# Where the spread of w_out's greatest row scale is written in an attention and feed-forward kernel

## The chip, the cores and the metric

One Trainium2 chip; the program runs on one of its cores. The metric is the device time of an execution in microseconds, and what stands for a kernel is the median of its runs. The kernel before was run three times: 697.34, 698.10 and 700.95 us.

## The reference, cut to what matters

```python
# B, H, S, D = 4, 8, 576, 64; d_model 512, d_ff 2048
x = (log1p(abs(i - j)) / log1p(max(i, 1)))[..., None]
bias = maximum(x @ w1 + b1, 0.0) @ w2              # one table for each head
scores = q @ k.T / 8 + bias
attn = exp(scores - scores.max(-1)); attn = attn / (attn.sum(-1) + 1e-9)
x = (attn @ v).transpose(0, 2, 1, 3).reshape(B * S, H * D)
h = x @ w_in                                       # w_in, w_out are float64
return ((h * clip(h + 3.0, 0.0, 6.0) / 6.0) @ w_out).astype(float32)
```

## The kernel before, in words

**Tiles and steps.** The attention is cut into 144 tiles of 128 query rows of one head, in pairs of heads: first the query columns 0 to 255 of all four batches (`u` = 0, four tiles for a pair), then the columns 256 to 575 (`u` = 1, five tiles). A loop at the end of the kernel function counts `n` from -1 to 150 (L1146). In turn n, `front(n)` writes the scores of tile n + 1, the row maximum of tile n, and what the tiles n - 1 to n - 6 still need; then come steps of the preparation of the weights, of the bias table and of the feed-forward part, and last `back(n)` with the exponential. The tiles of the batches 0 and 1 with u = 0 are computed in float32 and turned by TensorE (L614, L656); the others are split into high and low float16 parts and turned by DMA transposes on SP (L631).

**The feed-forward part.** `ffn(b, u)` is a generator (L728). It has 16 steps that each write 12 matmuls of `x @ w_in` into a PSUM tile `h_ps` (L773), with `post` (L745) turning an older `h_ps` into `t` (ScalarE L763, VectorE L756) and `g` (ScalarE L750, GpSimd L752). Then come 16 steps of 12 matmuls of `g @ w_out` into `o_ps` (L796), four for each of the four groups of output rows. The first one, `ffn(0, 0)`, stops between its halves with `yield "w2"` (L785): its second half needs the prepared `w_out`, and before the first `o_ps` it multiplies the sixteen `g` by the row ratios of `w_out` (L787, by turns on ScalarE L123 and VectorE L121).

**The preparation of w_out.** `w_out_prep` (L328) is a generator too. Its stages, for eight blocks k of two times 128 rows, are: load, sign (L256, L257), pack, split. `pack` (L354) shifts the float64 words together, takes the greatest value of each row (L264) and makes a power of two and its inverse of it (`row_scale`, L208, L163, L213). `split` (L359) writes the high and the low float16 parts into `wo`, the low ones on VectorE (L140). In the twelfth step only the split of block 7 is left. Behind the stages comes `row_ratio(pw, "w2")` (L215) with the chain of `spread_max` (L144) and a `yield` after each hop: a maximum over the eight scales of each partition on VectorE (`m_w`, L146); a transpose to one row on TensorE (L152); a maximum over that row on VectorE (`g_w`, L154); a product with a row of ones, which lays the value on all partitions, on TensorE (L156); a copy out of PSUM on VectorE (`p_w`, L159). Then VectorE takes the inverse (L218) and the ratios `r_w2c` (L220), and the tables of L371. The transpose and the product write the tile `m_ps`, which comes from the pool `w` like `h_ps`, `o_ps` and `pv_ps`; that pool has two PSUM banks at this stage.

**What sets the order.** A planner orders the instructions of each engine by their place in the text and by times that it reckons itself; it may let a later one pass where an earlier one isn't ready. From n = 45 on (`SWITCH`, the entry `sw`), `open_steady` (L1111) closes the PSUM pools, opens others with two and four tiles, and TensorE goes in the order of the text; SP too, from n = 45. An engine runs its own list in order in any case. How many steps a turn writes is kept in counters:

```python
ao[0] += cfg["ro"] if out_steps[0] < cfg["os"] else cfg["ro2"]     # 0.85, then 2.0 from 11 steps on
while ao[0] >= 1.0:
    ao[0] -= 1.0
    out_ready = not out_step()                                     # the generator is at its end
...
if phase == 1.5 and not out_ready:
    credit = cfg["gap"]                                            # 0.0
else:                            # rf0 1.3; rfo 2.3; rf 2.0, and rf1 1.55 from unit 16 on (u = 1)
    credit += cfg["rf0"] if phase == 1 else cfg["rfo"] if phase < 2 else ...
while credit >= 1.0 and queue and (phase < 2 or steady[0]):        # one feed-forward step for each
```

Phase is 1 from n = 21 (`START`), 1.5 while `ffn(0, 0)` stands at its `yield "w2"` and in its second half, and 2 when it is done; until n = 45 no other `ffn` is begun. Steps of the bias table (L855, L838, L842, L871) are written at 1.7 for a turn once `out_steps` has come to 12. What the queue of feed-forward steps holds at the end of the loop is written behind it.

Of the kernel before, what the change touches and what calls it, by code (L numbers as in the profile page):

```python
# [14 lines left out]
AF = mybir.ActivationFunctionType  # L15
# [9 lines left out]
NG = S // 16  # L25
CQ = 2.0 ** -25
VC = 5 * 128
CFG = {'z0': 'AD', 'gz': 12, 'z1': 'AD', 'gz2': 16, 'zeng': 'DDA', 'sg': 'P', 'wm1': 'A', 'wm2': 'RRAAAAAA', 'hl': 'AP', 'gl': 'PP', 'vm': 'A', 'g0': 8, 'rwi': 2.0, 'rw0': 0.3, 'rw1': 0.7, 'ro': 0.85, 'rb': 1.7, 'rf0': 1.3, 'rf': 2.0, 'rf1': 1.55, 'la': 6, 'gq': 2, 'gap': 0.0, 'wu': 8, 'act': 'o', 'g1': 2, 'w64': 5, 'rfo': 2.3, 'tv': 'A', 'pw': 0, 'po': 0, 'gr': 'AD', 'wb': 3, 'fb': 2, 'spn': 45, 'sw': 45, 'ws': 2, 'kn': 10, 'kw': 1, 'os': 11, 'ro2': 2.0, 'bo': 12, 'rb0': 1.5}
F64_BIAS = 2.0 ** -112
F64_MAX = float(np.uint32(0x0FEFFFFF).view(np.float32))  # L30

# [2 lines left out]
def attention_moe_kernel(  # L34
# [16 lines left out]
    nc = tc.nc  # L51
    cfg = CFG
# [4 lines left out]
    KF = DFF // 128  # L57
# [13 lines left out]
    stack_p = ctx.enter_context(ExitStack())  # L71

    def open_psum(stack, ns, nw):
        for tag, n in (("s", ns), ("w", nw)):
            pools["ps_" + tag] = stack.enter_context(
                tc.tile_pool(
                    name=f"ps_{tag}{n}", bufs=n, space=bass.MemoryType.PSUM, reuse_waits="tile"
                )
            )
# [4 lines left out]
    phase = 0  # L84
    out_open = [False, 0]
    steady = [False]
    queue = []

    def w_bank(name):

        if name == "o_ps":
            out_open[:] = [True, 0]
        elif out_open[0] and steady[0]:
            while out_open[0] and out_open[1] == 3:
                next(queue[0])
            out_open[1] += 1
        return pools["ps_w"].tile([128, 512], F32, tag="w", name=name)
# [109 lines left out]
    def row_scale(top, p, s):  # L207
        nc.vector.tensor_scalar(  # L208
            out=p.bitcast(U32), in0=top.bitcast(U32), scalar1=3, scalar2=0x7F800000,
            op0=ALU.logical_shift_left, op1=ALU.bitwise_and,  # L210
        )
        to_pow2(p)
        nc.vector.reciprocal(out=s, in_=p)  # L213

    def row_ratio(p, name):  # L215
        pm = yield from spread_max(p, name)
        rm = const.tile([128, 1], F32, name=f"rm_{name}")
        nc.vector.reciprocal(out=rm, in_=pm)  # L218
        r = const.tile([128, p.shape[1]], F32, name=f"r_{name}c")
        nc.vector.tensor_scalar(out=r, in0=p, scalar1=rm, scalar2=None, op0=ALU.mult)  # L220
        pscale[name] = pm
        pscale["r" + name[1]] = r
# [105 lines left out]
    def w_out_prep():  # L328
        top = const.tile([128, KF // 2], F32, name="w2top")
        pw = const.tile([128, KF // 2], F32, name="w2p")  # L330
        sw = const.tile([128, KF // 2], F32, name="w2s")

        def col(t, k):
            return t[:, k:k + 1]

        def load(k):
            src = w_out[256 * k:256 * k + 256, :].rearrange("(a p) e -> p a e", a=2)
            return f64_load(src, k)

        def load_early(k, _):  # L340
            return load(k) if k < 6 else None

        def load_late(k, t):
            return load(k) if k >= 6 else t

        def sign(k, t):
            if k % 2:
                u = const.tile([128, 2 * S], F32, tag="kb1", name="cu")
            else:
                u = pools["e"].tile([128, 2 * S], F32, tag="cu", name="cu")  # L350
            u = u[:, 0:1024]
            return (*f64_abs(t, u), u)

        def pack(k, tu):  # L354
            f64_pack(*tu[:3], col(top, k))
            row_scale(col(top, k), col(pw, k), col(sw, k))
            return tu[3].rearrange("p (k e) -> p k e", k=2)

        def split(k, u):  # L359
            ks = slice(2 * k, 2 * k + 2)  # L360
            for step in range(2):
                split_w(wo[:, 0, ks, :], wo[:, 1, ks, :], u, col(sw, k), step, pick("wm2", k))

        ws = cfg["ws"]
        yield from staged(KF // 2, [
            (0, load_early), (ws - 1, load_late), (ws, sign), (ws + 1, pack), (ws + 2, split),
        ])
        yield from row_ratio(pw, "w2")
        for name, c in (("t3", 3.0 * CQ), ("t6", 6.0 * CQ)):
            t = const.tile([128, KF // 2], F32, name=name)  # L370
            nc.vector.tensor_scalar(  # L371
                out=t, in0=pscale["r2"], scalar1=c, scalar2=None, op0=ALU.mult
            )
            pscale[name] = t
# [298 lines left out]
    def x_first(b, p):  # L673
        ps = pv_t.pop((b, p, 0))
        n = 256
        x = x_tile(b, 0)
        xr = hl_p.tile([128, 2, n], F32, tag="hl", name="xr")
        xs, rb = xr[:, 0], xr[:, 1]
        nc.scalar.activation(
            out=rb, in_=ps[:, 1, 0:n], func=AF.Copy,  # L680
            scale=pscale["x1"][:, p:p + 1] if b else pscale["v0"][1],
        )
        nc.vector.tensor_mul(out=xs, in0=ps[:, 0, 0:n], in1=rb)  # L683
        xh = x[:, 0, p]
        nc.scalar.activation(out=xh, in_=xs, func=AF.Copy)
        nc.gpsimd.tensor_sub(out=x[:, 1, p], in0=xs, in1=xh)
# [137 lines left out]
    bias_ps = {}  # L824
# [19 lines left out]
        bias_z[g] = zs  # L844

    def bias_mm(g):
        if steady[0]:
            pss = [w_bank("b_ps") for _ in range(2)]
        else:
            ps = s_bank("b_ps")  # L850
            pss = [ps[:, 0], ps[:, 1]]
        zs = bias_z.pop(g)
        for a in range(2):
            for k, z in enumerate(zs):
                nc.tensor.matmul(  # L855
                    out=pss[a][32 * k:32 * k + 32, 0:HALF], lhsT=w2_sb,
                    rhs=z[:, a * HALF:(a + 1) * HALF],
                )
        bias_ps[g] = pss if steady[0] else ps

    def bias_out(g):
        ps = bias_ps.pop(g)
# [59 lines left out]
    def front(n):  # L922
        late = at(n + 1) and not direct(*tiles[n + 1])
        if at(n + 1) and not late:
            qk_step(n + 1)
        if at(n):
            soft_max(n)
        if n == START:
            open_ffn()
        if n == SWITCH:  # L930
            open_steady()
        if late:
            qk_step(n + 1)
        if unit_at(n - 6):
            x_low(*unit_at(n - 6))
        if at(n - 1):
            soft_norm(n - 1)
        if at(n - 2):
            soft_low(n - 2)
            if tiles[n - 2][2] in (1, 3, 5, 7, 8):  # L940
                freed[0] += 1
        if at(n):
            aux(n)
        if at(n - 3):
            soft_turn(n - 3)
        if unit_at(n - 5):
            pv_step(*unit_at(n - 5))
        while len(bt_t) - freed[0] < 4 and len(bt_t) < len(keys):
            k, b, p, i = keys[len(bt_t)]
            if k - n > (cfg["la"] if n > 3 else 2):  # L950
                break
            bias_until(128 * i + 128 if i < 2 else S)
            bt_t[b, p, i] = load_bias(b, p, i)
        if unit_at(n - 6) and unit_at(n - 6)[1] == PAIRS - 1:
            return unit_at(n - 6)[::2]
        return None
# [95 lines left out]
    def drain(gen):  # L1052
        for _ in gen:
            pass
# [34 lines left out]
    def open_ffn():  # L1089
        nonlocal phase  # L1090
        drain(gen_w)
        hidden_scale(0)
        for c in range(KC):
            xv = x_t[0, 0][:, :, c]
            nc.vector.tensor_scalar(
                out=xv, in0=xv, scalar1=pscale["r1"][:, c:c + 1], scalar2=None, op0=ALU.mult
            )
        if cfg["fb"] > 1:
            x1 = const.tile([128, KC], F32, name="x1")
            nc.vector.tensor_scalar(  # L1100
                out=x1, in0=pscale["r1"], scalar1=pscale["v1"][1], scalar2=None, op0=ALU.mult
            )
            pscale["x1"] = x1
        stack_a.close()
        del pools["a"], pools["w"]
        pools["g"] = ctx.enter_context(tc.tile_pool(name="g", bufs=1, reuse_waits="tile"))
        pools["f"] = ctx.enter_context(tc.tile_pool(name="f", bufs=2, reuse_waits="tile"))
        queue.append(ffn(0, 0))
        phase = 1

    def open_steady():  # L1111
        nonlocal phase
        while phase < 2:
            ffn_step()
        stack_p.close()
        open_psum(ctx, 2, 4)
        steady[0] = True
        keep_order("PE")

# [121 lines left out]
```

## Time and profile before

| what | us |
|---|---|
| median of three runs | 698.10 |
| lowest and highest | 697.34, 700.95 |
| profiled execution | 701.47 |
| its span, first to last instruction | 699.7 |
| TensorE busy in the span | 643.5 (92%) |
| ScalarE, VectorE, GpSimd busy | 488.1, 481.9, 254.5 |

The profile is of one execution. PE stands for TensorE's matmuls, PEld for its weight loads, DVE for VectorE, ACT for ScalarE, POOL for GpSimd, SP for the queue that issues most DMAs. A releaser behind an arrow is the instruction that ended an idle time. PEclk is the granted clock as a share of the full one (1.00 is 2.4 GHz, 0.50 is 1.2 GHz). A few per cent of the matmul records can be missing.

### The profile page before, as it was taken

What the parts mean: (1) busy time and instruction counts of PE and PEld (TensorE: products, weight loads), DVE (VectorE), ACT (ScalarE), POOL (GpSimd) and SP (SyncE); (2) the same over time, 40 slices, a digit from 0 to 9 for tenths busy, and PEclk for the clock granted to TensorE, in tenths of its full rate; (3) what the DMA queues carried; (4) which work ended last, traced back from release to release, by engine and by line L of the source; (5) the groups of instructions that cost most, each with busy time, mean ns of one, the idle gap of its engine ahead of it and who ended that gap; (6) DMA issues with size and microseconds to landing.
All of it is one profiled execution on the core that took longest, in us unless ns stands there. A gap on an engine that the chain in (4) does not pass through costs nothing. (4 is left out here: it accounts for less than half of the span.)

```text
span 699.7 us, 15119 instructions
## 1 busy us (share of the span) xinstructions
PE 643.5 (92%) x5558; PEld 456.8 (65%) x5558; DVE 481.9 (69%) x1157; ACT 488.1 (70%) x963; POOL 254.5 (36%) x322
## 2 busy tenths in 40 slices
PE   7687899775999999999898899999999999999998
PEld 2233556552576667688787788767776777777775
DVE  7989868899757786667777877777678767410310
ACT  7987778886657897677668876886678856621620
POOL 1112126774202444045434552565236512410420
PEclk9999999998799999999999999999999999999999
DMA  8899679643798949999999799969796877100000
GB/s 297 298 363 344 242 277 330 217 166 77 218 256 201 246 82 299 189 237 180 244 262 250 142 229 184 219 147 200 139 243 121 161 151 128 21 10 29 1 10 28
DMA packets 175737, 130.13 MB, mean 186 GB/s; under 512 B 137520, under 2 KB 144944, under 8 KB 174640
## 3 DMA queue, kind: packets, MB, share of 16 engines
q1 hardware_dynamic: 165872, 113.84, 65.0%
q10 hardware_dynamic: 9792, 15.34, 7.2%
q8 instruction: 43, 0.70, 0.4%
q14 instruction: 30, 0.25, 0.1%
HBM read 77.24 MB, written 15.34 MB: 132 GB/s over the span
## 5 line engine op out<-in xcount | busy, mean ns | idle before, releaser
L773 PE MATMUL h_ps<-x,wi 128*128 128x256 f16 (+1 forms) x1536 | 200.7, 289 | 15.1 <-DVE xr L683 7.4
L796 PE MATMUL o_ps<-g,wo 128*128 128x256 f16 (+1 forms) x1536 | 195.5, 286 | 1.0 <-ACT g L123 1.0
L773 PEld LDWEIGHTS <-wi 128*128 128x128 f16 x1536 | 148.0, 99 | 63.4 <-issue 21.8
L796 PEld LDWEIGHTS <-wo 128*128 128x128 f16 x1536 | 147.2, 98 | 46.9 <-issue 9.9
L752 POOL TENSOR_TENSOR g<-t,g 128x256 f16<-128x256 f32 (+1 forms) x128 | 100.4, 795 | 127.9 <-ACT g L750 126.9
L566 ACT ACTIVATE bt<-bt,sm 128x576 f32<-128x576 f32 x144 | 110.5, 768 | 51.2 <-DVE sm L555 49.0
L140 DVE SCALAR_TENSOR_TENSOR hl<-bt,sm,hl 128x576 f16<-128x576 f32 x112 | 98.6, 893 | 24.9 <-ACT hl L123 14.3
L756 DVE SCALAR_TENSOR_TENSOR t<-t,t,h_ps 128x320 f32<-128x320 f32 (+1 forms) x112 | 56.3, 515 | 66.3 <-ACT t L763 65.1
L117 POOL TENSOR_SCALAR hl<-bt,sm 128x576 f16<-128x576 f32 x56 | 45.9, 821 | 105.9 <-DVE sm L578 52.6
L750 ACT ACTIVATE g<-t 128x256 f16<-128x256 f32 (+1 forms) x128 | 55.4, 440 | 35.9 <-DVE t L756 35.2
L555 DVE CUSTOM_DVE_ANT_0 bt<-s_ps,bt 128x576 f32<-128x576 f32 x88 | 64.4, 750 | 11.8 <-PE s_ps L543 6.5
L763 ACT ACTIVATE t<-h_ps,t,hr 128x320 f32<-128x320 f32 (+1 forms) x112 | 64.6, 586 | 8.2 <-PE h_ps L773 6.9
L409 POOL TENSOR_TENSOR qkl<-st,qkh 128x576 fp32r<-128x576 f32 (+2 forms) x48 | 57.2, 1214 | 32.0 <-ACT qkh L402 26.5
L855 PE MATMUL b_ps<-z_e,w_sb 128*32 128x288 f32 x448 | 47.6, 445 | 8.5 <-ACT z_e L842 3.3
L806 ACT ACTIVATE ot<-o_ps,os 128x256 f32<-128x256 f32 (+1 forms) x32 | 15.9, 496 | 56.7 <-PE o_ps L796 54.4
L123 ACT ACTIVATE hl<-bt,sm 128x576 f16<-128x576 f32 x56 | 43.0, 769 | 5.3 <-issue 1.2
L574 DVE TENSOR_SCALAR sm<-sm 128x1 f32<-128x1 f32 x112 | 16.8, 150 | 43.2 <-ACT bt L566 42.9
L838 DVE TENSOR_SCALAR z_e<-T,nbp 128x576 f32<-128x576 f32 x69 | 37.4, 586 | 5.4 <-PE b_ps L855 5.2
L543 PE MATMUL s_ps<-qkh 64*128 64x288 f32 x192 | 30.9, 353 | 8.9 <-DVE sm L555 7.3
L842 ACT ACTIVATE z_e<-T,bp 128x576 f32<-128x576 f32 x43 | 32.2, 770 | 6.6 <-PE b_ps L855 2.9
L871 ACT ACTIVATE bo<-b_ps,cv_sb,isc 128x576 f32<-128x576 f32 (+1 forms) x47 | 33.3, 711 | 3.8 <-PE b_ps L855 2.7
L257 POOL TENSOR_SCALAR w<-w 128x1024 f32<-128x1024 f32 x8 | 11.8, 1472 | 63.0 <-ACT wo L256 57.0
(132 smaller groups left out, 891.2 us busy)
## 6 DMA issues: line engine op xcount, KB each, us to landing
bt<-bias SPq DMA_DIRECT2D x36, 576.0 KB, 5.4
bias<-bo ACTq DMA_DIRECT2D x36, 288.0 KB, 5.6
w<-in_w_in_dram SPq DMA_DIRECT2D x8, 1024.0 KB, 7.0
vs<-in_vp_dram SPq DMA_DIRECT2D x24, 320.0 KB, 5.2
st<-in_qk_dram SPq DMA_DIRECT2D x16, 448.0 KB, 4.5
wo<-in_w_out_dram SPq DMA_DIRECT2D x5, 1024.0 KB, 6.6
bt<-bias SPq DMA_DIRECT2D x16, 288.0 KB, 3.5
qk<-in_qkd_dram SPq DMA_DIRECT2D x8, 544.0 KB, 8.7
```

The lines of the kernel that those rows point to most:

```text
L117: nc.gpsimd.tensor_scalar(out=out, in0=full, scalar1=scale, scalar2=1.0, op0=ALU.mult, op1=ALU.mult)
L140: nc.vector.scalar_tensor_tensor(out=out, in0=full, scalar=scale, in1=high, op0=ALU.mult, op1=ALU.subtract)
L409: nc.gpsimd.tensor_sub(out=lo[:, c:c + w], in0=t[:, c:c + w], in1=hi[:, c:c + w].bitcast(F32))
L555: nc.vector.tensor_tensor_reduce(out=halves(bt), in0=ps, in1=halves(src), op0=ALU.add, op1=ALU.min, scale=-0.125, scalar=3.0e38, accum_out ...
L566: nc.scalar.activation(out=bt, in_=bt, func=AF.Exp, scale=-1.0, bias=sm[:, 0:1], accum_out=total)
L750: nc.scalar.activation(out=g[:, 0], in_=uu, func=AF.Copy)
L752: e.tensor_sub(out=g[:, 1], in0=uu, in1=g[:, 0])
L756: nc.vector.scalar_tensor_tensor(out=t_t[f], in0=t_t[f], scalar=cols(f)[2], in1=h_t.pop(f)[:, 0:n], op0=ALU.min, op1=ALU.mult,)
L763: nc.scalar.activation(out=t_t[f], in_=h_t[f][:, 0:n], func=AF.Relu, scale=cols(f)[0], bias=cols(f)[1],)
L773: nc.tensor.matmul(out=h_t[f][:, 0:n], lhsT=wi[:, a, c, f * 128:(f + 1) * 128], rhs=x[:, e, c], start=(k == 0), stop=(k == 3 * KC - 1),)
L796: nc.tensor.matmul(out=ops[:, 0:n], lhsT=wo[:, a, f, e * 128:(e + 1) * 128], rhs=g_t[f][:, r], start=(f == 0 and a == 0 and r == 0), stop= ...
L855: nc.tensor.matmul(out=pss[a][32 * k:32 * k + 32, 0:HALF], lhsT=w2_sb, rhs=z[:, a * HALF:(a + 1) * HALF],)
```

## The change

The row-ratio chain of `w_out` is made a generator in `pack` of the last block and drained there, so it is written in the eleventh step of `w_out_prep`, before the step with the last split. At its old place the generator is at its end and gives no more `yield`. The other new names do nothing with the values given: `psw` = 99 calls `open_banks` in a turn in which it has been called, `xp` = 0 takes the old branch, and `four` is set in the same call as `steady`.

```diff
-CFG = {..., 'bo': 12, 'rb0': 1.5}
+CFG = {..., 'bo': 12, 'rb0': 1.5, 'psw': 99, 'xp': 0, 'mw': 2}
...
+        ratio = []
...
         def pack(k, tu):
             f64_pack(*tu[:3], col(top, k))
             row_scale(col(top, k), col(pw, k), col(sw, k))
+            if k == KF // 2 - 1 and cfg["mw"]:
+                ratio.append(row_ratio(pw, "w2"))
+                if cfg["mw"] > 1:
+                    drain(ratio[0])
+                else:
+                    next(ratio[0])
             return tu[3].rearrange("p (k e) -> p k e", k=2)
...
-        yield from row_ratio(pw, "w2")
+        yield from ratio[0] if ratio else row_ratio(pw, "w2")
...
-        elif out_open[0] and steady[0]:
+        elif out_open[0] and four[0]:
...
+        if n == cfg["psw"]:
+            open_banks()
         if n == SWITCH:
             open_steady()
...
+    def open_banks():
+        if not four[0]:
+            stack_p.close()
+            open_psum(ctx, 2, 4)
+            four[0] = True
...
     def open_steady():
         nonlocal phase
         while phase < 2:
             ffn_step()
-        stack_p.close()
-        open_psum(ctx, 2, 4)
+        open_banks()
         steady[0] = True
         keep_order("PE")
```

## Rows read from the trace of the kernel before

**Rows 1.** The page: busy time, share of the span and instructions of each engine.

```profile
PE 643.5 (92%) x5558; PEld 456.8 (65%) x5558; DVE 481.9 (69%) x1157; ACT 488.1 (70%) x963; POOL 254.5 (36%) x322
```

**Rows 2.** Windows, all engines; the last three columns are granted clock, DMA share, GB/s.

```profile
core 0: us, PE busy (x) PEld busy (x) DVE busy (x) ACT busy (x) POOL busy (x), PEclk, DMA share, GB/s
169.00:182.00 13.00, 12.03 (x57) 6.12 (x58) 10.33 (x23) 7.31 (x13) 5.54 (x7) 0.50 0.97 278
...
190.00:223.00 33.00, 32.78 (x315) 24.48 (x312) 23.33 (x62) 21.92 (x40) 5.83 (x7) 1.00 0.88 226
223.00:233.00 10.00, 8.36 (x93) 4.72 (x93) 7.33 (x17) 7.41 (x13) 3.20 (x4) 0.84 1.12 220
233.00:300.00 67.00, 64.00 (x678) 48.13 (x676) 46.98 (x108) 54.70 (x112) 24.85 (x33) 1.00 0.87 205
300.00:440.00 140.00, 132.31 (x1302) 110.97 (x1300) 107.84 (x267) 103.28 (x232) 63.93 (x95) 0.99 0.99 218
440.00:618.00 178.00, 175.93 (x1488) 127.55 (x1487) 123.41 (x305) 127.92 (x270) 76.91 (x105) 1.00 0.72 146
```

**Rows 3.** Timeline 169 to 189 us: start, duration, engine, line, what, count, idle before.

```profile
169.42 2.72 PE L773 MATMUL h_ps<-x,wi 128*128 128x256 f16 x12 [5.86 <-DVE xr L683]
...
170.95 0.14 DVE L146 TENSOR_REDUCE m_w<-w2p 128x1 f32<-128x8 f32 x1
...
173.39 1.27 DVE L140 SCALAR_TENSOR_TENSOR wo<-cu,w2s,wo 128x1024 f16<-128x1024 f32 x1
...
174.15 0.37 PE L152 MATMUL m_ps<-eye_sb,m_w 128*1 128x128 f32 x1
...
175.84 0.27 DVE L154 TENSOR_REDUCE g_w<-m_ps 1x1 f32<-1x128 f32 x1
...
183.81 0.38 PE L156 MATMUL m_ps<-g_w,ones_sb 1*128 1x1 f32 x2
...
184.22 0.16 DVE L159 COPY p_w<-m_ps 128x1 f32<-128x1 f32 x1 [3.53 <-PE m_ps L156]
...
184.79 0.22 DVE L220 TENSOR_SCALAR r_w2c<-w2p,rm_w 128x8 f32<-128x8 f32 x1
...
188.86 3.33 PE L796 MATMUL o_ps<-g,wo 128*128 128x256 f16 x29 [1.04 <-ACT g L123]
```

**Rows 4.** Windows of 2 us, TensorE alone: busy, granted clock, DMA share, GB/s.

```profile
184.00:186.00 2.00, 1.84 (x17) 1.00 0.00 0
186.00:188.00 2.00, 1.81 (x16) 1.00 0.03 8
188.00:190.00 2.00, 1.14 (x11) 1.00 0.75 136
...
226.00:228.00 2.00, 1.35 (x17) 1.00 1.65 160
228.00:230.00 2.00, 1.01 (x11) 0.94 0.59 201
230.00:232.00 2.00, 2.00 (x17) 0.50 0.86 206
232.00:234.00 2.00, 2.00 (x17) 0.71 1.08 172
...
336.00:338.00 2.00, 2.00 (x17) 0.50 1.12 262
338.00:340.00 2.00, 2.00 (x27) 0.75 1.23 234
```

**Rows 5.** Timeline of TensorE behind the switch at n = 45.

```profile
232.21 8.05 PE L773 MATMUL h_ps<-x,wi 128*128 128x256 f16 x68
```

**Rows 6.** Timeline of TensorE, two idle times of the ordered part.

```profile
262.07 2.78 PE L773 MATMUL h_ps<-x,wi 128*128 128x256 f16 x24 [1.66 <-DVE t L756]
...
335.82 0.85 PE L543 MATMUL s_ps<-qkh 64*128 64x288 f32 x3 [2.43 <-DVE sm L555]
```

**Rows 7.** Groups of TensorE's instructions, 618 to 700 us: busy, mean ns, idle.

```profile
L796 PE MATMUL o_ps<-g,wo 128*128 128x320 f16 x384 | 52.5, 299 | 0.0
L773 PE MATMUL h_ps<-x,wi 128*128 128x320 f16 x193 | 26.5, 299 | 0.0
```

**Rows 8.** Groups of VectorE and ScalarE, 235 to 300 us: busy, mean ns, idle, releaser.

```profile
L756 DVE SCALAR_TENSOR_TENSOR t<-t,t,h_ps 128x256 f32<-128x256 f32 x16 | 7.6, 478 | 6.0 <-ACT t L763 5.8
...
L763 ACT ACTIVATE t<-h_ps,t,hr 128x256 f32<-128x256 f32 x16 | 8.7, 556 | 1.6 <-PE h_ps L773 1.2 <-ACT g L750 0.3
L750 ACT ACTIVATE g<-t 128x256 f16<-128x256 f32 x16 | 6.4, 413 | 1.8 <-DVE t L756 1.6
```

More of the change, by code (lines that the diff above doesn't have):

```diff
@@ L27 @@
 VC = 5 * 128
-CFG = {'z0': 'AD', 'gz': 12, 'z1': 'AD', 'gz2': 16, 'zeng': 'DDA', 'sg': 'P', 'wm1': 'A', 'wm2': 'RRAAAAAA', 'hl': 'AP', 'gl': 'PP', 'vm': 'A', 'g0': 8, 'rwi': 2.0, 'rw0': 0.3, 'rw1': 0.7, 'ro': 0.85, 'rb': 1.7, 'rf0': 1.3, 'rf': 2.0, 'rf1': 1.55, 'la': 6, 'gq': 2, 'gap': 0.0, 'wu': 8, 'act': 'o', 'g1': 2, 'w64': 5, 'rfo': 2.3, 'tv': 'A', 'pw': 0, 'po': 0, 'gr': 'AD', 'wb': 3, 'fb': 2, 'spn': 45, 'sw': 45, 'ws': 2, 'kn': 10, 'kw': 1, 'os': 11, 'ro2': 2.0, 'bo': 12, 'rb0': 1.5}
+CFG = {'z0': 'AD', 'gz': 12, 'z1': 'AD', 'gz2': 16, 'zeng': 'DDA', 'sg': 'P', 'wm1': 'A', 'wm2': 'RRAAAAAA', 'hl': 'AP', 'gl': 'PP', 'vm': 'A', 'g0': 8, 'rwi': 2.0, 'rw0': 0.3, 'rw1': 0.7, 'ro': 0.85, 'rb': 1.7, 'rf0': 1.3, 'rf': 2.0, 'rf1': 1.55, 'la': 6, 'gq': 2, 'gap': 0.0, 'wu': 8, 'act': 'o', 'g1': 2, 'w64': 5, 'rfo': 2.3, 'tv': 'A', 'pw': 0, 'po': 0, 'gr': 'AD', 'wb': 3, 'fb': 2, 'spn': 45, 'sw': 45, 'ws': 2, 'kn': 10, 'kw': 1, 'os': 11, 'ro2': 2.0, 'bo': 12, 'rb0': 1.5, 'psw': 99, 'xp': 0, 'mw': 2}
 F64_BIAS = 2.0 ** -112
@@ L86, in attention_moe_kernel @@
     steady = [False]
+    four = [False]
     queue = []
@@ L682, in x_first @@
         )
-        nc.vector.tensor_mul(out=xs, in0=ps[:, 0, 0:n], in1=rb)
+        if cfg["xp"]:
+            nc.scalar.activation(out=xs, in_=ps[:, 0, 0:n], func=AF.Copy)
+            nc.gpsimd.tensor_mul(out=xs, in0=xs, in1=rb)
+        else:
+            nc.vector.tensor_mul(out=xs, in0=ps[:, 0, 0:n], in1=rb)
         xh = x[:, 0, p]
@@ L846, in bias_mm @@
     def bias_mm(g):
-        if steady[0]:
+        if four[0]:
             pss = [w_bank("b_ps") for _ in range(2)]
@@ L858, in bias_mm @@
                 )
-        bias_ps[g] = pss if steady[0] else ps
+        bias_ps[g] = pss if four[0] else ps
     def bias_out(g):
```

## The prediction

> **What bounds the kernel now.** I read the page first: TensorE is busy 92% of the span, the next engines 70% [rows 1]. A share over the whole span says little of one stage, so the windows come next. From 190 to 223 us TensorE is busy 32.78 of 33 us, and from 440 us on nearly always; what it leaves idle behind the switch lies between 233 and 440 us, 3.0 + 7.7 us, and 2.1 more up to 618 us [rows 2]. There the kernel can be faster only by less idle time or less half-rate time of TensorE, whose work is the same before and after. Around the change the timeline shows how late the second half of the first feed-forward unit starts. The last maximum over the scales, m_w, is ready at 171.09 us, the ratios r_w2c at 185.01, the first o_ps product comes at 188.86 [rows 3]. So the chain of five small instructions takes 14 us.
>
> **The chain itself.** Nothing is added or removed: the same two TensorE visits and the VectorE operations, about 0.14 + 0.37 + 0.27 + 0.38 + 0.16 + 0.17 (the inverse, taken like the copy) + 0.22 = 1.7 us of work, and no DMA. Moved in front of the last split they pass, on VectorE, that split's low part (1.27 us at 173.39) and what stands between the yields [rows 3]. Their duration I cost at nothing, since it is work in both kernels. What is removed is waiting. The product L156 could have run behind g_w at 176.11 but ran at 183.81, 7.7 us later, and VectorE stood 3.53 us on it with everything else queued behind the copy [rows 3]. What isn't removed is the wait in front of the transpose: m_ps needs one of two banks of the pool w, which an h_ps and a pv_ps hold, so I leave it at 174.15. Then g_w at some 174.6, the product at 175 to 176 and r_w2c by about 177. From r_w2c to the first o_ps it took 3.9 us before; so o_ps starts near 179 to 181, eight to ten us earlier.
>
> **What the early start is worth.** Little by itself: TensorE wasn't waiting for it, it did other work. Between 184 and 190 us it was idle for 0.16 + 0.19 + 0.86 = 1.2 us [rows 4]; before that, from 169 to 182 us, it was busy 12.03 of 13 us at half clock [rows 2]. I take **-1.2 us** (bounds -1.2 and 0). The 3.53 us that VectorE no longer stands still let the attention run ahead; later TensorE waits 0.65 + 0.99 us for attention and bias at 226 to 230 us [rows 4], and half of that I give to it: **-0.8** (0 to -1.6).
>
> **The counters.** They move more than the chain does. By the code, w_out_prep makes 0.85 steps a turn from n = 21 on, so its eleventh falls in n = 33 (13 turns x 0.85 = 11.05); then two a turn. Before, its end is the sixteenth call, in n = 36; after, three yields are gone, the end is the thirteenth call, in n = 34. The sixteen h_ps steps at 1.3 a turn are out by n = 33, so o_ps steps are written in n = 36 to 42 before and 34 to 40 after. While phase 1.5 waits the credit is set to 0; in phase 2 it adds up until n = 45. Hence at n = 45 the credit was 6.4 and is now 10.3: six steps in one piece before, ten after. The trace bears out the six: one run of 68 recorded matmuls of 72 [rows 5]. From there every step lies four earlier in the text, and 43 instead of 47 are left behind the loop.
>
> **What that costs.** Between the end of o_ps and n = 45 there are now four turns without feed-forward work instead of two. The two took most of 223 to 233 us, with TensorE busy 8.36 of 10 [rows 2]. Two more of the kind: **+1.6** idle. The clock row bounds it from above: behind the short idle times at 226 to 230 us the grant was 0.50 for 2 us and 0.71 for 2 more, which loses 1.0 + 0.6 us [rows 4]; so 0 to +3.3. The Trainium skill, "TensorE: Matmul & The Clock Gate", section "What's actually happening", says that the throttled state is the default and activity releases it; by it the added stretch falls to the half rate once more, and this term would be +3.3 instead of +1.6, the sum -1.7 instead of -3.4. The trace agrees so far: 0.50 behind those idle times [rows 4].
>
> **What it may give.** At 333.4 to 335.8 us TensorE stands 2.43 us, longest of the ordered part, for a scores bank that VectorE frees late [rows 6], and the clock is 0.50 and 0.75 for 2 us each behind it, 1.0 + 0.5 us lost [rows 4]. By the counters this is n = 68, the first tiles with u = 1, where the last h_ps steps of ffn(2, 0) fall. An h_ps step loads VectorE with 0.48 and ScalarE with 0.97 us [rows 8]; an o_ps step behind the first group loads neither. After the change those steps are over at n = 65, so VectorE is relieved of 4 x 0.48 = 1.9 us just ahead. Between 1.9 us and all of 2.43 + 1.5 = 3.9 I take **-3.0**; bounds -3.9 and 0.
>
> **The rest.** The wait of 1.66 us at 260.4 us has the same cause inside ffn(1, 0) [rows 6]; the ten steps at n = 45 move it, they needn't shrink it: 0, bounds -1.7 and +1.7. The four steps that leave the end would be 4 x 12 x 0.137 = 6.6 us there (26.5 us over 193 [rows 7]), but they are done earlier by the same busy engine: 0; bound -6.6, if all of it falls into time idle now. The renamed flags and the other entries do nothing.
>
> **Sum.** -1.2 - 0.8 + 1.6 - 3.0 = -3.4 us. The profiled execution took 701.47 us (699.7 of span and 1.8 around it), so 698.1 for its like; it lay 3.4 above the median of 698.1, and by the median the forecast is 694.7 us.
>
> **Rivals.** (A) **The loop has room for the four steps**: the 10.7 us idle between 233 and 440 us [rows 2] take them in, as the early burst lets VectorE and ScalarE clear what is late. Then -1.2 + 1.6 - 6.6 = -6.2: 691.9 us. For it: those idle times are waits for VectorE [rows 6]. Against: TensorE goes in order there, and a later wait isn't filled by work done earlier. (B) **The move comes to nothing**: the transpose still waits for its bank, the planner lets the pv products pass L156 as before, and the new shift only places the same idle times elsewhere; or the chain, written inside ffn's last h_ps steps, keeps a bank from h_ps for as long as it saves. 698.1 within 1.5 us. For it: TensorE is full from 190 to 223 us whatever the order [rows 2]. (C) **The gap behind o_ps decides against it**: four turns without filler at 223 to 233 us cost the full 3.3 us and the burst of ten, 4 x 1.34 = 5.4 us longer (8.05 us for six [rows 5]), holds back the scores so that the attention behind it makes TensorE stand once more by the longest kind of wait, 2.4 [rows 6], while n = 68 gains nothing. With the 1.2 saved: -1.2 + 3.3 + 2.4 = +4.5, 702.6 us. It decides from 4.7 us of idle and lost clock beyond what is there now (3.5 + 1.2). For it: the half rate has followed such gaps before [rows 4]. The Trainium skill's rule of the clock named above is the mechanism of its first part.
>
> **How the numbers follow.** A measurement of this kernel can tell about 0.5% from no change, 3.5 us. The forecast's case has 0.46, between 691 and 698.5; its middle lies at that bound, so 0.24 faster and 0.22 the same. A has 0.18, all faster. B has 0.17, all the same. C has 0.19, all slower. Faster 0.42, same 0.39, slower 0.19. The range goes from 690.0, somewhat below A, to 702.6, the price of C, and leaves out half of C and the ends of A.
>
> **What the profile after would show.** Right: m_w to r_w2c in 6 to 8 us instead of 14, no wait of VectorE on L156 over 1 us, first o_ps before 182 us, its last before 216; one run of ten h_ps steps behind the switch; idle at n = 68 under 1 us without half clock; some 43 steps in the tail. Wrong: r_w2c still behind 183 us (B); TensorE idle by 5 us or more, or at 0.50 for long, ahead of the run of h_ps steps (C); idle between 233 and 440 us down by 5 us (A). The whole forecast falls if the run at n = 45 isn't ten steps long.

## The result, and the profile after

The change makes the kernel slower: 705.72 us (seven runs, 703.41 to 709.83) against 698.10 (seven runs, 697.34 to 700.95), a ratio of 1.010 with a 95% interval of 1.0076 to 1.0124. That is 11.0 us above the forecast of 694.7 and 3.1 above the upper end of the range. The profiled execution took 703.41 us, with 701.6 of span; it is the quickest of the seven, while that of before, 701.47, lies above all seven of its runs. So the two profiles differ by 1.9 us and the medians by 7.6; a second profile of each kernel stands among the experiments.

The page of the kernel after, busy time by engine, as [rows 1]:

```profile
PE 643.9 (92%) x5558; PEld 455.8 (65%) x5558; DVE 485.6 (69%) x1157; ACT 488.1 (70%) x963; POOL 261.8 (37%) x322
```

The number of instructions is the same on every engine. Windows of the kernel after, all engines, columns as in [rows 2]:

```profile
169.00:182.00 13.00, 11.77 (x80) 5.98 (x82) 12.76 (x39) 9.82 (x16) 5.53 (x4) 0.83 1.01 269
182.00:190.00 8.00, 8.00 (x78) 5.83 (x77) 3.15 (x8) 5.97 (x12) 3.34 (x4) 1.00 0.65 163
190.00:223.00 33.00, 31.47 (x323) 22.76 (x320) 24.24 (x59) 20.66 (x37) 6.10 (x7) 1.00 0.78 209
223.00:233.00 10.00, 5.03 (x42) 2.65 (x38) 6.02 (x18) 4.67 (x8) 2.29 (x3) 0.75 1.11 218
233.00:300.00 67.00, 64.87 (x672) 49.16 (x669) 45.15 (x103) 52.17 (x107) 23.77 (x31) 0.99 0.78 190
300.00:440.00 140.00, 132.59 (x1279) 109.54 (x1277) 106.59 (x260) 102.30 (x227) 66.52 (x92) 0.98 0.98 211
```

From 182 to 190 us TensorE has no gap any more; that is the early start. What it won is gone behind that: from 190 to 223 us TensorE works 31.47 of 33 us instead of 32.78, and from 223 to 233 us 5.03 of 10 instead of 8.36 [rows 2].

The timeline of the kernel after around the chain, columns as in [rows 3] (L147, L153, L155, L157, L160 and L221 are the old L146, L152, L154, L156, L159 and L220; h_ps is L786, o_ps L809, s_ps L552):

```profile
168.13 0.41 DVE L696 TENSOR_TENSOR xr<-pv_ps,xr 128x256 f32<-128x256 f32 x1
...
170.12 0.14 DVE L147 TENSOR_REDUCE m_w<-w2p 128x1 f32<-128x8 f32 x1
...
170.23 1.17 PE L868 MATMUL b_ps<-z_e,w_sb 128*32 128x288 f32 x4 [7.49 <-POOL x L699]
...
171.33 0.37 PE L153 MATMUL m_ps<-eye_sb,m_w 128*1 128x128 f32 x1
...
172.56 0.27 DVE L155 TENSOR_REDUCE g_w<-m_ps 1x1 f32<-1x128 f32 x1
...
173.55 1.48 PE L786 MATMUL h_ps<-x,wi 128*128 128x256 f16 x12
...
174.96 0.38 PE L157 MATMUL m_ps<-g_w,ones_sb 1*128 1x1 f32 x2
...
175.54 0.14 DVE L160 COPY p_w<-m_ps 128x1 f32<-128x1 f32 x1
...
175.87 0.53 PE L552 MATMUL s_ps<-qkh 64*128 64x288 f32 x2
...
176.41 0.22 DVE L221 TENSOR_SCALAR r_w2c<-w2p,rm_w 128x8 f32<-128x8 f32 x1
...
179.54 0.50 PE L809 MATMUL o_ps<-g,wo 128*128 128x256 f16 x3
```

From the start of m_w to the end of r_w2c it takes 6.5 us instead of 14.1, VectorE no longer waits for the product, and o_ps starts 9.3 us earlier. But the order on TensorE is another: the transpose stands in front of the last h_ps of ffn(0, 0), not behind it. That h_ps starts 5.4 us after xr (168.13) instead of right behind its xr [rows 3].

Further down, the timeline of TensorE alone in the kernel after, behind 199 us and around the switch:

```profile
199.99 0.53 PE L552 MATMUL s_ps<-qkh 64*128 64x288 f32 x4
...
209.09 1.48 PE L809 MATMUL o_ps<-g,wo 128*128 128x256 f16 x12
...
229.48 0.84 PE L552 MATMUL s_ps<-qkh 64*128 64x288 f32 x3 [4.97 <-ACT bo L884]
...
233.29 13.98 PE L786 MATMUL h_ps<-x,wi 128*128 128x256 f16 x120
...
251.03 0.53 PE L552 MATMUL s_ps<-qkh 64*128 64x288 f32 x4
```

The last o_ps ends at 210.6 us. The run behind the switch has ten steps (120 matmuls, none missing here) instead of six [rows 5]. Windows of 2 us of the kernel after, TensorE alone, columns as in [rows 4]:

```profile
224.00:226.00 2.00, 0.51 (x2) 1.00 1.85 190
226.00:228.00 2.00, 0.00 (x0) 0.99 0.64 179
228.00:230.00 2.00, 0.52 (x4) 0.50 1.03 248
230.00:232.00 2.00, 2.00 (x19) 0.50 0.92 170
232.00:234.00 2.00, 2.00 (x16) 0.50 1.02 229
234.00:236.00 2.00, 2.00 (x17) 0.81 0.98 311
```

TensorE stands nearly still for 6 us, and behind that the grant is 0.50, which is 1.2 GHz, up to 234 us. The Trainium skill, "TensorE: Matmul & The Clock Gate", section "What's actually happening", has the throttled state as the default that activity releases; the rows agree, with 0.50 behind the standstill and 0.81 at 234 to 236 us, once TensorE has been busy from 230 us on.

**Where the time goes, stretch by stretch.** I cut the timelines of TensorE at the first score matmul of four turns: P0 (near 152 us), P1 (near 176, the scores around the chain), P2 (near 198, the next ones), P3 (the first full ones behind the switch), then at the last pv product, and at the end. P3 is the same tile in every kernel. All kernels of the table reach P0 alike (150.8 to 154.8 us, with no order between them). Durations in us, worked out from the starts:

```
                                P0-P1  P1-P2  P2-P3  P3-pv  pv-end
before                           24.6   21.9   46.4  366.1   89.1
before, second profile (e8)      24.0   19.2   45.7  369.1   89.1
after                            25.1   24.1   51.0  368.0   82.6
after, second profile (e12)      25.2   24.1   51.2  368.3   82.6
yields back (e1)                 26.3   18.3   47.8  367.8   89.1
ten steps, chain as before (e4)  23.4   19.2   51.0  374.8   82.6
after, run of six (e3)           25.1   24.1   45.8  366.7   89.1
o_ps spread (e17)                26.4   22.9   42.4  365.3   89.1
yields back, switch 43 (e10)     25.0   18.3   48.2  366.1   89.1
o_ps spread, switch 43 (e18)     25.6   22.9   41.8  365.3   89.1
```

By the means of two profiles each, the kernel after loses 0.8 + 3.6 + 5.1 + 0.6 us in four stretches and wins 6.5 in the last: +3.5 us of span. The medians differ by more, 7.6 us; the rest isn't placed by these four profiles, but most of it by all of them together (at the end of the experiments).

### The profile page after: what moved, and what is told of

Same layout as the page of the kernel before. It is cut to its first block, busy times and chain, and to the rows that moved or that the text cites. A ratio compares the mean times of both kernels' runs of the same rounds, so it can differ in the third digit from the quotient of the medians.

```text
span 701.6 us, 15111 instructions
## 1 busy us (share of the span) xinstructions
PE 643.9 (92%) x5558; PEld 455.8 (65%) x5558; DVE 485.6 (69%) x1157; ACT 488.1 (70%) x963; POOL 261.8 (37%) x322
## 5 line engine op out<-in xcount | busy, mean ns | idle before, releaser
L786 PE MATMUL h_ps<-x,wi 128*128 128x256 f16 (+1 forms) x1536 | 200.1, 288 | 6.8 <-DVE x L141 3.3
L809 PE MATMUL o_ps<-g,wo 128*128 128x256 f16 (+1 forms) x1536 | 196.0, 286 | 1.1 <-POOL g L765 1.1
L786 PEld LDWEIGHTS <-wi 128*128 128x128 f16 x1536 | 147.9, 98 | 55.3 <-issue 12.9
L809 PEld LDWEIGHTS <-wo 128*128 128x128 f16 x1536 | 147.2, 98 | 47.7 <-issue 10.6
L765 POOL TENSOR_TENSOR g<-t,g 128x256 f16<-128x256 f32 (+1 forms) x128 | 104.2, 825 | 123.6 <-ACT g L763 122.9
L769 DVE SCALAR_TENSOR_TENSOR t<-t,t,h_ps 128x320 f32<-128x320 f32 (+1 forms) x112 | 56.2, 516 | 66.0 <-ACT t L776 64.7
L418 POOL TENSOR_TENSOR qkl<-st,qkh 128x576 fp32r<-128x576 f32 (+2 forms) x48 | 61.1, 1293 | 38.0 <-ACT qkh L411 31.0
L564 DVE CUSTOM_DVE_ANT_0 bt<-s_ps,bt 128x576 f32<-128x576 f32 x88 | 64.6, 751 | 14.4 <-PE s_ps L552 7.9
L868 PEld LDWEIGHTS b_ps<-z_e,w_sb 128*32 128x32 f32 x448 | 15.4, 114 | 37.4 <-DVE z_e L851 8.0
L552 PE MATMUL s_ps<-qkh 64*128 64x288 f32 x192 | 30.0, 349 | 8.3 <-ACT bo L884 5.0
```

Of the source, the lines that this page charges most:

```text
L418: nc.gpsimd.tensor_sub(out=lo[:, c:c + w], in0=t[:, c:c + w], in1=hi[:, c:c + w].bitcast(F32))
L552: nc.tensor.matmul(out=s_t[n + j][:, a, 0:HALF], lhsT=w[q], rhs=m[rows, cs], start=(k == 0), stop=(k == 2),)
L564: nc.vector.tensor_tensor_reduce(out=halves(bt), in0=ps, in1=halves(src), op0=ALU.add, op1=ALU.min, scale=-0.125, scalar=3.0e38, accum_out ...
L765: e.tensor_sub(out=g[:, 1], in0=uu, in1=g[:, 0])
L769: nc.vector.scalar_tensor_tensor(out=t_t[f], in0=t_t[f], scalar=cols(f)[2], in1=h_t.pop(f)[:, 0:n], op0=ALU.min, op1=ALU.mult,)
L786: nc.tensor.matmul(out=h_t[f][:, 0:n], lhsT=wi[:, a, c, f * 128:(f + 1) * 128], rhs=x[:, e, c], start=(k == 0), stop=(k == 3 * KC - 1),)
```

## The experiments

Of two kernels a second profile was taken. The first is the file of after with the chain at its old place; its trace has as many instructions on every engine as that of before, and with these values the other new names do nothing. The second is the kernel after, as it is.

```diff
-'mw': 2
+'mw': 0        # e8; e12 has no edit
```

> The changed text with mw at 0, which gives the instruction lists of the kernel before on every engine. One more profile of it, to see how the time between the first instruction and the run of h_ps steps, and behind it, varies between executions. Both theories: 697 to 702 us, the run beginning at 230 to 233 us.

> The changed kernel once more, one profile. Its first profile was of its fastest execution. Both theories: 703 to 709 us; the first scores of tile 36 later than 176 us if the chain's place costs before them, and 549 to 551 us less from there to the end... the second part alone: 525 us or more from those scores to the end, against 523 in the two profiles of the kernel before.

Measured: 702.99 (1 us above its range) and 708.06 us, one run each. Both fill the table above. P1 to P2 varies by 2.7 us within the kernel before, and by nothing (24.1, 24.1) after. The clock explains it: over this stretch the first profile of before was granted 0.87 of the full rate, which loses 0.13 x 21.9 = 2.9 us, e8 and both profiles of after 1.00. At 1.00 all five profiles with the chain and its yields at the old place (e8 and, from the experiments below, e4, e6, e15 and e16) take 19.0 to 19.2 us, so the loss there is 4.9 us rather than the 3.6 of the means. The lines of TensorE in e8 at P1 and at P2, and its group of o_ps between them:

```profile
178.06 0.53 PE L552 MATMUL s_ps<-qkh 64*128 64x288 f32 x2
...
197.28 0.53 PE L552 MATMUL s_ps<-qkh 64*128 64x288 f32 x4
```

```profile
L809 PE MATMUL o_ps<-g,wo 128*128 128x256 f16 x72 | 8.2, 273 | 0.9 <-ACT g L124 0.9
```

**The chain's place apart from the counters.** First the chain at its new place with three empty yields at the old one, so the counters are those of before; then the opposite, the chain in one piece at its old place, with the counters of after.

```diff
-        yield from ratio[0] if ratio else row_ratio(pw, "w2")
+        for _ in range(3):                       # e1
+            yield
-        yield from ratio[0] if ratio else row_ratio(pw, "w2")
+        drain(row_ratio(pw, "w2"))               # e2, with 'mw': 0
```

> The changed kernel with three empty yields at the chain's old place: the chain stands early in one piece, the counters are those of before (o_ps in turns 36 to 42, a run of six h_ps steps at n = 45). If the counters cost the time: 698 us within 2, no wait of TensorE over 3 us between 215 and 233 us. If the chain's new place costs it (it passes the last split and what VectorE has queued): 703 to 708 us, as the changed kernel.

> The kernel before with the chain written without yields at its old place, behind the last split: the counters are those of the changed kernel (o_ps two turns earlier, a run of ten h_ps steps), the chain isn't moved. If the counters cost the time: 703 to 708 us, with TensorE idle for 8 us or more between 190 and 233 us. If the chain's new place costs it: 698 us within 2.

Measured: e1 1.003 (1.000 to 1.006), e2 1.0184 (1.0149 to 1.0219). So some 0.7 of the 1.0% goes with the yields, and at most 0.6% with the place. e1 with 701.13 us lies between its two ranges. e2 with 712.02 lies above its 703 to 708, with 3.3 us of idle TensorE from 190 to 233 us instead of the 8 expected; why it is slower than the change is open. With the yields gone, the new place is even the better one, 1.010 against 1.018. What the yields do is seen between P1 and P2. The groups of TensorE's instructions by line from P1 to P2, first of the kernel after, then of e1 (its L810 is the same line):

```profile
L809 PE MATMUL o_ps<-g,wo 128*128 128x256 f16 x132 | 15.1, 273 | 0.0
```

```profile
L810 PE MATMUL o_ps<-g,wo 128*128 128x256 f16 x76 | 9.0, 273 | 0.0
```

In both kernels TensorE has no idle time worth naming there. The change puts 15.1 instead of 9.0 us of o_ps in front of the scores at P2, 6.1 us more, and P1 to P2 is 24.1 instead of 18.3, 5.8 us more (the other groups nearly cancel; the bias products take 4.6 instead of 5.4 us). All seven profiles with the chain at the new place in pool w and o_ps written from n = 34 at 2.3 a turn (after, e12, e3, e5, e7, e11, e13) have 23.9 to 24.1.

**The turns without filler, and the run of ten.** The kernel after with the credit held so that the run has six steps; before with four steps more in the run; after with feed-forward steps allowed from n = 41 on.

```diff
+            if n < SWITCH:                       # e3
+                credit = min(credit, 4.4)
+            if n == SWITCH:                      # e4, with 'mw': 0
+                credit += 4.0
-            while credit >= 1.0 and queue and (phase < 2 or steady[0]):
+            while credit >= 1.0 and queue and (phase < 2 or steady[0] or n >= 41):   # e7
```

> The changed kernel with the credit held to 4.4 until n = 45, so that the run at the switch is six steps as before; o_ps stays two turns early, four turns without feed-forward work. If those turns without filler cost the time: 703 to 708 us still. If the longer run and the shift of all later steps by four cost it: 697 to 700 us. If both: between 700 and 703 us.

> The kernel before with 4 added to the credit at n = 45: a run of ten steps and every later step four earlier, as in the changed kernel, but o_ps in its old turns and the chain in its old place. If the turns without filler cost the time: 698 us within 2. If the longer run and the shift cost it: 702 to 708 us. If the loop has room for four steps: 691 to 695 us.

> The changed kernel with feed-forward steps allowed from n = 41 on, ahead of the switch: the h_ps steps of ffn(1, 0) are written two a turn into the four empty turns, the switch stays at 45. If the turns without filler cost the time: 694 to 700 us, idle before n = 45 under 3 us. If the planner's order with two banks for h_ps and pv_ps costs as much as the filler gains: 703 us or more.

Measured: e3 1.0104 (1.0071 to 1.0137), e4 1.0067 (1.0039 to 1.0095), e7 1.0054 (1.0026 to 1.0083). With six steps P2 to P3 goes back to 45.8 us and the tail to 89.1: the run of ten costs about 5 us there and gives 6.5 back in the tail, and by the times of e3 and after (1.0104 and 1.010) the kernel after isn't slower for it. e3 against e1 is the plainest test of the early start: both have the chain at its new place and six steps at the switch, and differ in the turns of o_ps and the empty ones behind it (and in the place of the small tables behind the chain). In the same comparison they take 705.91 and 701.13 us, 4.8 us apart. In e4 the same trade of run and tail came out as a loss; its profile shows 374.8 us between P3 and the last pv, 6 to 10 more than the others of the table, with the clock at 0.94 to 0.98 up to 440 us (0.97 to 1.00 in the profiles of before and after), and why is open. Filling the empty turns brings back about half of the loss, though e7's 704.94 us lie outside the 694 to 700 expected of it.

**The switch moved.** The same kernels with the switch at n = 43, where the old counters leave no empty turn and the new ones two, and at n = 41, where the new ones leave none.

```diff
-'sw': 45
+'sw': 43       # e5 after; e6 before ('mw': 0); e10 as e1
+'sw': 41       # e11 after
```

> The changed kernel with the switch (sw) at n = 43 instead of 45: two turns without feed-forward work between the end of o_ps and the first h_ps step instead of four, as in the kernel before. If the turns without filler cost the time: the idle time of TensorE between o_ps and the run of h_ps steps falls from 6.5 us to under 3, the run begins before 230 us, and the time is 696 to 700 us. If the early o_ps costs it in another way (order, banks, the shift of the later steps): 703 us or more.

> The kernel before with the switch at n = 43: no turn without feed-forward work is left between o_ps and the run. If such turns cost time there too: 1.5 to 4 us less than before, 694 to 697 us. If the switch sets only the place of the work: 698 us within 2. It is the control of the run with the switch at 43 in the changed kernel.

> The chain early, the three empty yields at its old place (the counters of before), and the switch at n = 43: no turn without feed-forward work, no step earlier than before. If the loss is the sum of the empty turns and of the chain's place, it stands against the kernel before with the switch at 43 (0.8% under before) as the chain with yields stands against before (0.3% over): 0.3 to 0.6% under before. If the chain's place is free there: 0.8% under before.

> The changed kernel with the switch at n = 41: o_ps two turns early, but h_ps steps follow it at once, and all later steps lie four earlier against the tiles. If the empty turns cost the time, it goes on falling from 1.0% (four) over 0.5% (two) to within 0.3% of before. If the shift by four steps costs by itself: 0.5% over before or more, as with two empty turns.

Measured: e5 1.0048 (1.0016 to 1.008), whose 703.11 us lie above the 696 to 700 expected if the empty turns alone cost it; e6 0.992 (0.9882 to 0.9957), the best ratio of all and ahead of both kernels, though its medians, 696.13 against 699.91 us, make only 0.995; e10 0.9961 (0.9935 to 0.9986); e11 0.9998 (0.9967 to 1.0029). With the changed kernel four, two and no empty turns ahead of the switch measure 1.010, 1.005 and 1.000, though the switch itself moves along. By the ratios the new place of the chain is the worse one here as well (e10 against e6), but the intervals overlap, and the medians of e10 make 0.994, so this isn't shown.

**The bank of the transpose.** m_ps of w_out taken from the pool of the scores.

```diff
-        ps = w_bank("m_ps")
+        ps = s_bank("m_ps")[:, 0] if name == "w2" else w_bank("m_ps")
```

> The changed kernel with the small tile m_ps of w_out's chain taken from the pool s instead of the pool w, so that the transpose can't take the bank for which the last h_ps of ffn(0, 0) waits. If that bank is part of the cost: the last h_ps starts within 0.7 us behind the xr product as before (instead of 5 us behind it), and the time is 2 to 3 us under the changed kernel's 705.7. If the order of the small instructions doesn't matter: 704 us or more, as the changed kernel.

Measured: 1.013 (1.009 to 1.0171), no gain. The timeline of TensorE in it shows why the time says little of the bank:

```profile
169.09 1.95 PE L786 MATMUL h_ps<-x,wi 128*128 128x256 f16 x12 [3.84 <-DVE xr L696]
175.43 0.37 PE L153 MATMUL m_ps<-eye_sb,m_w 128*1 128x128 f32 x1 [4.40 <-DVE m_w L147]
175.74 0.85 PE L552 MATMUL s_ps<-qkh 64*128 64x288 f32 x4
```

The last h_ps starts right behind its xr again, which fits the bank as what held it back. But the transpose now waits 4.40 us for m_w, and behind it stand the scores that every other kernel writes near 152 us (P0) and that come here at 175.74. So the order differs by far more than a bank, and the run doesn't tell what the bank costs.

**Who multiplies g.** Seen in the traces: the eight multiplications of g by the ratios on ScalarE (5.0 us, from 176.74 us on in the kernel after, 188.09 before) now run ahead of two exponentials. Four kernels give them to VectorE.

```diff
-'gr': 'AD'
+'gr': 'D'      # e13 after; e14 as e1; e15 before; e16 as e6
```

> The changed kernel, with the eight multiplications of g by the row ratios that ScalarE did given to VectorE. In the changed kernel they take ScalarE for 5.0 us from 176.74 us on, as soon as the ratios are there, and the two exponentials of the tiles whose scores were made at 175.9 to 178.5 us come behind them (182.44, 185.31), where before they came ahead (2.7 us behind the first score). Theory (these multiplications hold back the attention, and the turns behind inherit it): exponentials some 2 to 5 us earlier against the first score, the scores of the next pair 2 to 4 us earlier against it (24.1 us behind it in the changed kernel), ratio to before 1.005 to 1.008 instead of 1.010. Rival 1 (the bank that the transpose takes from h_ps, and the empty turns, explain all): 1.010 whatever ScalarE does. Rival 2 (VectorE is as tight as ScalarE there): the second row maximum waits 2.2 us more and nothing is won, 1.010 or more.

> The chain at its new place with the three empty yields at the old one (counters as before; it measured 1.003), and the eight multiplications of ScalarE given to VectorE. Theory: the move's own cost was these multiplications in front of two exponentials, so 0.999 to 1.001. Rival 1 (it was the bank): 1.003. Rival 2: 1.003 or more.

> Control: the instruction order of before, with the same eight multiplications given to VectorE. There the exponentials run ahead of them on ScalarE. All theories: within 0.2% of before (2.2 us more on VectorE, 5.0 us less on ScalarE at 188 us, with TensorE idle 1.04 us for the first g at most).

> The order of before with the switch at n = 43 (it measured 0.992), and the eight multiplications given to VectorE. All theories: 0.990 to 0.993; under 0.990 if ScalarE's 5 us count there too.

Measured: 1.0077 (1.0045 to 1.0109), 1.0045 (1.0018 to 1.0072), 0.9984 (0.9957 to 1.0011), 0.9939 (0.9909 to 0.9969). The theory gets little support: e13 has a time in its range, but P1 to P2 stays at 23.9 us, where 2 to 4 less were expected, and e14 misses its 0.999 to 1.001 and isn't better than e1. The controls, e15 and e16, lie within their intervals of what was expected. The timeline of VectorE in e13 shows that the trial isn't clean either, the sixteen multiplications stand between the two row maxima (L564):

```profile
179.69 0.76 DVE L564 CUSTOM_DVE_ANT_0 bt<-s_ps,bt 128x576 f32<-128x576 f32 x1 [0.35 <-PE s_ps L552]
...
180.65 4.28 DVE L122 TENSOR_SCALAR g<-g,r_w2c 128x512 f16<-128x512 f16 x16
...
186.87 0.74 DVE L564 CUSTOM_DVE_ANT_0 bt<-s_ps,bt 128x576 f32<-128x576 f32 x1
```

Still, it decides what P1 to P2 hangs on: in e14 the second exponential comes at 187.18 us, 9.1 behind P1, and P2 comes 18.6 behind P1; in e1 it comes 10.3 behind and P2 18.3, in the kernel after 9.4 and 24.1. It is TensorE's list, not the exponentials.

**The same start, spread out.** The kernel after with 1.8 instead of 2.3 steps of ffn(0, 0)'s second half in a turn: o_ps begins in n = 34 and ends in n = 42 as before; then with the switch at 43 as well.

```diff
-'rfo': 2.3
+'rfo': 1.8     # e17; e18 with 'sw': 43
```

> The changed kernel with 1.8 instead of 2.3 steps a turn for the second half of the first feed-forward unit, so its o_ps steps, which still begin in n = 34, end in n = 42 as before instead of n = 40, with two turns without filler, and six steps at the switch instead of ten. Theory (the o_ps steps, put two turns earlier into a TensorE that is full, hold back the next pair of scores by their own time, and what is missing behind them leaves it idle): the scores of the pair behind 176 us come 20 to 22 us behind that pair's instead of 24.1, TensorE is busy over 8 of the 10 us from 223 us on, ratio 1.002 to 1.006. Rival 1 (the chain drained in one piece costs it, wherever o_ps lies): 1.010. Rival 2 (any early start of o_ps costs it): 1.008 to 1.010.

> The same with the switch at n = 43, behind which no turn is empty. Theory: as with the three yields back and that switch, 0.994 to 0.998. Rivals: 1.000 or more (that of the changed kernel with a switch at 43 was 1.0048).

Measured: e17 1.0055 (1.0034 to 1.0077), inside its range, though P1 to P2 with 22.9 us stays above the 20 to 22 that were expected. Half of the loss goes with the crowding and the empty turns, the chain, the start of o_ps and the run of six being as in e3 (1.0104). The window of TensorE before the switch in e17 is as busy as before (8.36) again, columns as in [rows 4]:

```profile
223.00:233.00 10.00, 8.43 (x105) 1.00 1.15 220
```

e18 measured 1.0048 (1.002 to 1.0075) and missed its 0.994 to 0.998. In it P2 still comes 22.9 us behind P1, in e10 18.3; both end o_ps in n = 42 and have no empty turn, and differ in where its steps begin. By the ratios, then, an o_ps that begins in n = 34 costs by itself, but the profiles don't show where. What e18 loses up to P2 it has won back at P3: P1 to P3 is 64.7 us in e18 and 66.5 in e10, and likewise 65.3 in e17 and 66.1 in e1. By these profiles a late P2 is a loss only where the stretch behind it doesn't make it good; in e3, with o_ps crowded, P1 to P3 is 69.9.

**All profiles together.** Nineteen profiles place more of the loss than the two pairs do (all but e9, where P0's scores come behind the transpose). P0 to P1 takes 23.2 to 24.6 us in the seven with the chain at its old place and 25.0 to 26.9 in the twelve with the new one, 23.72 and 25.75 on the mean: the place costs some 2.0 us. P1 to P2 loses 4.9 us, as above, and P2 to P3 5.1 by the two pairs. P3 to the last pv takes 367.7 to 374.8 us (mean 369.4) in the eight kernels whose later steps lie four earlier, and 360.7 to 369.1 (mean 365.6) in the other eleven: 3.7 us, the least sure of the terms, as the two groups overlap. With the 6.5 us won in the tail that makes +9.2 us, where the medians say +7.6; each profile is a single execution, and their clocks differ.

## Why the prediction was wrong, point by point

**The chain itself.** Right in its time: 6.5 us from m_w to r_w2c, forecast 6 to 8; the copy doesn't wait. Wrong in "I leave it at 174.15": the transpose came at 171.33. It came ahead of the last h_ps, it seems in the bank that xr had just freed (e9 fits that), and that h_ps started at 173.55 instead of 169.42. Costed at 0, the place shows as 0.8 us to P1 in the two pairs of profiles, 1.7 to 2.3 in e1 against before, and 2.0 by all profiles; in e1's runs the whole move costs 0 to 0.6%. The forecast named this only as a neutral part of B.

**What the early start is worth.** This is the step that failed first. The 1.2 us of idle time from 184 to 190 us did go (8.00 of 8 busy), and I booked them as a gain. But TensorE is full from 190 to 223 us [rows 2], so o_ps written two turns earlier goes ahead of something. It went ahead of the scores at P2: 6.1 us more of it there, P2 5.8 us later against e1, 4.9 against the old order at full clock (e8 and four more), and 4.8 us of time between e3 and e1. I had used "TensorE is full" to say that the start is worth little, and not that it has a price.

**The counters.** Right in every count: first o_ps at 179.54, last at 209.09, ten steps behind the switch, and a tail of four steps less (82.6 instead of 89.1 us from the last pv to the end).

**What that costs.** Mis-sized, +1.6 with a bound of +3.3. From the end of o_ps to the run at the switch TensorE stood 6.5 us instead of 1.6: 8.36 - 5.03 = 3.3 us more from 223 to 233 us, most of the rest from 190 to 223 us. The half rate behind it took 1.0 + 1.0 + 0.4 us from 230 to 236 us, where it took 1.0 + 0.6 before [rows 4], so about +5.7 together. Rival C had 3.3 for it. But it isn't paid again at P3: between P2 and P3 e3, with the same empty turns and six steps, takes 45.8 us, no longer than before. In this order the attention sets the pace there. The 4.97 us of TensorE end with `bo` on ScalarE, and ScalarE itself stands for transfers before it, by its timeline in the kernel after:

```profile
224.29 0.83 ACT L124 ACTIVATE vh<-vs,s_v 128x640 f16<-128x640 f32 x1 [1.35 <-DMA vs<-in_vp_dram]
...
227.26 0.78 ACT L124 ACTIVATE hl<-bt,sm 128x576 f16<-128x576 f32 x1 [2.14 <-DMA at<-hl]
...
228.62 0.81 ACT L884 ACTIVATE bo<-b_ps,cv_sb,isc 128x576 f32<-128x576 f32 x1
```

Taking o_ps out of the attention's way there hurries it little: 45.8 us in e3 against 45.7 and 46.4 before, and 47.8 in e1. So the empty turns are, for the most part, o_ps's 5.8 us a second time, seen from behind: paid at P2, not won back. It isn't a floor of the attention, though, for with o_ps spread (e17) the same stretch takes 42.4 us; why not in e3 is open.

**VectorE's 3.53 us (-0.8).** Nothing came of it: the idle time at 226 to 230 us that I halved grew from 0.65 + 0.99 [rows 4] to 2.00 + 1.48 us, and the wait of the scores there from 1.6 us, by the view of waits of the kernel before, to 4.97:

```profile
PE s_ps L543 <- ACT bo L871: 1.6, 1, 1.6
```

**What it may give (-3.0).** The waits of TensorE for the row maxima did shrink. From 160 to 440 us, by the views of waits of the kernel before and after (total, times, longest):

```profile
PE s_ps L543 <- DVE sm L555: 4.8, 3, 2.4
```

```profile
PE s_ps L552 <- DVE sm L564: 2.4, 3, 1.2
```

At n = 68 they are 0.64 and 0.59 us instead of 2.43 [rows 6]. But between them TensorE now stands 1.06 us for a `g` of GpSimd, which the earlier o_ps asks for, and the half clock comes behind it all the same. The timeline of TensorE in the kernel after, and its windows of 2 us behind it:

```profile
337.04 0.53 PE L552 MATMUL s_ps<-qkh,tq 128*128 128x288 f32 x2 [0.64 <-DVE sm L564]
...
341.57 0.38 PE L809 MATMUL o_ps<-g,wo 128*128 128x256 f16 x2 [1.06 <-POOL g L765]
...
342.87 0.53 PE L552 MATMUL s_ps<-qkh 64*128 64x288 f32 x3 [0.59 <-DVE sm L564]
```

```profile
344.00:346.00 2.00, 2.00 (x22) 0.50 1.19 289
346.00:348.00 2.00, 2.00 (x18) 0.65 1.37 211
```

So 2.29 us of idle time stand for 2.43, and 1.0 + 0.7 us of lost clock for 1.0 + 0.5 [rows 4]. P3 to the last pv is 368.0 and 368.3 us against 366.1 and 369.1: nothing of the 3.0 is left.

**The four steps at the end (0).** They are worth 6.5 us there, as the row of the tail said, and cost some 5 in the run of ten, which holds P3 back; P3 to the last pv, with every later step earlier, is longer by 3.7 us on the mean of all profiles. I had set all of it to nothing.

**Rivals and signs.** C, with 0.19, had the sign and the nearest price, 702.6; of its two parts the gap was there, and the burst held the scores back, but by e3's time the burst isn't what decides. The sign that I set for C, TensorE idle by 5 us or more or at 0.50 for long ahead of the run, is what the trace shows. The sign at n = 68, idle under 1 us without half clock, failed. A fell: the idle time between 233 and 440 us went from 10.7 to 9.5 us, not by 5. B fell with the ratio. None of the rivals had o_ps ahead of the scores at P2.

**The sum, term by term.** The forecast had 0 for the place of the chain, -1.2 for the early start, -0.8 for VectorE, +1.6 for the empty turns, -3.0 for n = 68 and 0 for the four steps: -3.4. The profiles have +2.0, +4.9 (the empty turns being the same time seen from behind), nothing for VectorE and n = 68, and 5.1 + 3.7 - 6.5 = +2.3: +9.2, against +7.6 in the medians.

**What stays open.** e4's slow stretch behind the switch; what e2 and e18 lose; why the stretch from P2 to P3 makes up for a late P2 in e17 and not in e3; and how the 0.3% of the chain's new place splits between the bank and the order of TensorE's list.

## What to carry to other kernels

Where an engine is full, work that becomes ready earlier isn't free: look what it overtakes in that engine's list, and price it at its own duration for whatever sets the pace behind, unless the stretch behind makes it good. A `yield` in a generator that is stepped at a rate is a delay by design; taking it away shifts everything counted behind it, and that shift can outweigh the waits that the edit removes. Try the shift alone (empty yields) and the edit alone before judging either; here the best order, 0.8% ahead of before by the ratio and 0.5% by the medians, keeps the old chain and moves one counter, the switch, two turns forward.

## What the runs showed of the hardware that was not expected

The same instruction lists run at different granted clocks in the same stretch. The last h_ps but one of ffn(0, 0), twelve matmuls, took 1.48 us at 162.08 us in the profile of before (granted 1.00 from 162 to 164 us) and 2.74 at 165.87 in e8's (0.50 from 165.8 to 168.6). From P1 to P2 it was the other way round (0.87 and 1.00), and the two profiles of one kernel differ by 2.7 us there (21.9 and 19.2), as much as the changes compared here. Runs of one kernel spread over 3.6 us here (before, seven runs) and over 6 to 10 in the larger comparisons (17 to 32 runs), so an interval, not a pair of runs, is needed for half a per cent.
